# A fused attention and feed-forward kernel on one core: a new hand-stored instruction order, with some copies moved to other engines and one batch's transposes moved to TensorE

## The chip, the cores and the metric

The kernel runs on one core of one Trainium2 chip. The metric is the device time of one launch in microseconds, the median of several runs. A profile of a single execution comes with it; its span runs from the first to the last instruction, and the time of that execution is a little longer than its span.

## What is computed

Linear attention with an exponential feature map, followed by a feed-forward layer with a squared ReLU:

```python
def phi(x):
    proj = np.einsum('bhsd,df->bhsf', x, w_phi)
    proj = proj - np.max(np.abs(proj), axis=-1, keepdims=True)
    return np.concatenate([np.exp(proj), np.exp(-proj)], axis=-1)
q_p, k_p = (phi(q), phi(k))
kv = np.einsum('bhsf,bhsd->bhfd', k_p, v)
z = np.sum(k_p, axis=2)
num = np.einsum('bhsf,bhfd->bhsd', q_p, kv)
den = np.einsum('bhsf,bhf->bhs', q_p, z)[..., None] + 1e-06
x = (num / den)              # to tokens x 512
out = maximum(x @ w_in, 0)**2 @ w_out
```

There are 8 batches of 8 heads, 576 positions and 64 channels per head, 128 features; 4608 tokens, model width 512, hidden width 2048. Inputs and output are float32, and the matmuls take bf16.

## The kernel before

One batch of attention is loaded at a time by GpSimd's DMA queue, which also casts to bf16: `xk`, `xv`, `xq` (L346). For batch 0 the loads are split, k0 into three (the third is half of it). The weights `win` (L364) and `wout` (L369) are loaded in two halves each. A batch's 36 units of 64 positions by two heads are handled in five groups: four of 8 units and one of 4.

Per batch:
- k and q are transposed to `kT` and `qT`. For batches 0 and 1 this is done by TensorE against an identity (L425) with a copy out of PSUM: k by L438 on DVE, or L441 on ACT for the groups below `KTD` of batch 0, and q by L433 on DVE. For later batches SP issues a transposing DMA (L414).
- the features of k: a 64-row matmul with `wphi` (L483), the largest absolute value on DVE (L494), and exponentials on ACT into `kph`. There are two ways. The first `FG` groups of batches 0 and 1 take the exponential straight from PSUM (L527, 512 wide, four per group), and put the scale on v instead: a small exponential (L534) and a multiply on GpSimd (L542) make two scaled `va`. The other groups subtract the maximum on DVE into `ksh` (L504) and take the exponential from there (L512, two per group); their `va` is a plain copy with a column of ones (L465, L466).
- `kv` by 64-row matmuls (L575), in two halves of heads (hf 0 and hf 1), copied by ACT or DVE (L590, L594). A half is issued as four lots of 18 matmuls.
- per pair of position blocks: the features of q (L621, exponentials L628 on ACT; L653 and a maximum on DVE, L660 or L674, then a small exponential), then numerator and denominator (L721), and a scale, a reciprocal and a product on DVE (L731, L738, L742) into `xo`.
- each 128 tokens of `xo` are transposed to `xT`: for batches below `XPE` by TensorE (L752) with a copy by ACT (L757), for the others by a transposing DMA that SP issues (L761).

The feed-forward part runs through nine chunks of 512 tokens: `ffn_in` (L783, then ReLU on ACT L788 and the square on GpSimd L791, or DVE L794 for the last chunks), and `ffn_out` (L814, sixteen 512-column matmuls per 128 tokens in four parts, copied out by DVE L831 and stored by SP L836). For chunk 0 the first `ffn_in` groups cover 128 tokens each, so that they can start as soon as one `xT` is there.

The order of the work is not that in which the code states it. The code makes a list of numbered operations, each with an engine, and `ORDER` is a table of all their numbers. `play` goes through this table and issues each operation; so the table fixes each engine's own order, and with it which ring buffer each operation gets. A negative number −n in the table stands for n warm-up matmuls (L379) that compute nothing. The table holds 56 of them, 55 ahead of the first `ffn_in` group. Costs, due times and pacing edges in the code (such as `pl.after`) were used in making the table; they don't add instructions. The waits between engines follow from which buffers the operations read and write.

In the old table, ahead of the first `xT` copy (L757), ACT has 1 kT copy, 12 L527, 6 L534, 2 full and 2 half L512, 16 L628, 2 L590 and 2 L668.

Of the kernel before, what the change touches and what calls it, by code (L numbers as in the profile page):

```python
# [44 lines left out]
class Plan:  # L45
# [48 lines left out]
    7 9 11 13 15 6 1 2 8 10 17 4 5 -17 35 -2 37 36 38 19 12 52 53 56 -1 63 54 65 55 68 -2 43 39 41 40 -2 74 64  # L94
    69 59 70 42 18 76 75 66 77 58 81 67 80 83 57 -2 85 86 87 44 72 78 79 88 89 -14 45 90 46 92 20 -1 49 50 47
    48 -4 107 112 111 91 93 128 131 114 113 -2 133 134 135 61 94 132 129 110 130 109 108 14 16 21 71 51 23 73
    25 82 60 -4 97 95 84 62 103 96 98 102 175 27 29 31 100 115 136 22 33 104 99 101 106 149 176 177 105 150 151
    24 385 26 137 116 138 -1 142 121 139 170 117 118 122 143 123 119 140 141 120 124 125 144 145 152 171 172
    153 174 173 -3 196 197 146 126 127 154 155 198 156 191 147 148 1442 178 199 1443 193 194 192 -1 210 211
    1435 28 1448 214 215 236 237 225 157 195 1449 179 180 238 226 227 239 240 1445 1446 245 243 184 185 1451  # L100
    387 1444 1450 389 1452 231 230 181 212 1436 158 213 186 163 1437 241 232 229 246 1447 244 1454 182 183 159
    164 160 165 187 188 161 166 162 167 30 32 247 248 249 1439 242 1455 228 234 1438 1456 1440 200 168 169 263
    264 189 250 190 265 1441 1457 254 256 252 253 251 1458 258 201 259 205 1464 1460 1463 1465 266 267 1453 235
    233 255 1461 257 206 260 262 261 216 202 218 207 220 217 219 208 268 270 269 271 221 327 388 222 209 203
    204 280 1467 273 272 1462 224 1459 1466 223 328 284 282 283 329 281 275 285 286 287 274 277 301 330 304 288
    276 279 278 306 302 307 308 309 303 305 34 1471 289 1475 294 1482 290 295 1476 1483 322 310 315 323 325 324
    326 311 296 291 316 297 292 298 293 1478 317 312 318 319 313 314 386 299 320 321 300 390 391 393 401 407
    405 403 1490 336 348 350 349 337 1479 1491 1480 343 345 3 347 346 344 1492 1486 1481 331 338 339 364 366
    369 1485 371 370 367 368 351 372 365 1489 357 1472 1493 1494 1468 352 1473 1474 1503 1469 1470 1504 1505
    1484 358 359 1514 332 340 353 333 354 334 355 360 356 361 378 379 335 1487 1500 1499 373 374 1501 1515 1502  # L110
    413 1516 1488 394 392 419 414 416 409 404 402 410 406 408 411 415 1496 380 1506 1510 375 420 376 381 377
    421 1513 1517 412 559 1511 1497 417 1518 418 1520 1521 382 395 396 1507 478 479 424 425 480 473 426 1498
    1512 561 1523 1529 1536 422 423 475 1508 476 477 563 1509 1524 474 427 428 397 341 362 398 429 431 430 363
    1543 342 1537 1544 1538 1477 399 1522 383 400 434 435 500 1550 502 1551 501 1525 481 482 1539 1545 1546
    1519 433 432 1553 1554 436 562 1540 1541 438 437 442 456 439 458 457 441 451 445 440 443 452 454 444 448
    446 447 495 449 453 450 1526 1577 483 488 484 489 560 1555 587 503 499 1527 459 498 460 455 496 497 504
    1542 1528 1552 1495 384 1581 485 1585 490 486 491 487 492 1547 505 510 461 506 511 462 1533 466 507 512 513
    467 1534 463 464 508 1530 468 1548 1531 1549 1535 1532 1589 564 567 565 577 581 575 493 509 514 515 469 465
    470 471 579 568 1590 544 517 520 522 518 521 524 546 523 545 519 566 1559 1563 593 594 595 588 539 494 472
    516 583 576 578 582 580 584 585 525 526 543 541 547 1595 1599 548 1567 542 540 549 554 532 527 1603 589 596  # L120
    597 1607 533 555 534 528 529 556 1571 590 1574 591 1575 535 1608 550 557 536 1572 530 592 1564 1565 551 552
    553 558 531 1582 1583 1576 586 735 1578 630 632 625 628 626 569 570 598 599 1566 1584 737 1586 631 1579 629
    627 1604 1587 1605 600 1606 1580 739 1588 602 571 573 1609 1573 1591 537 572 1568 574 652 653 608 603 604
    605 738 1560 1561 601 1613 1617 1569 1570 654 606 1600 1601 655 1602 633 1556 1557 1592 607 610 609 612 611
    614 674 616 613 676 675 677 1562 1558 620 615 618 617 622 619 1593 621 624 634 678 647 669 671 670 656 673
    623 672 736 740 743 741 538 1621 635 1625 636 637 1618 638 1626 639 684 640 679 641 1610 642 685 1596 757
    651 648 649 650 643 680 644 645 1619 657 658 681 682 662 686 663 687 1614 688 683 659 664 660 665 1631 763
    1597 1594 1620 1615 1611 1612 1598 666 661 696 698 691 718 697 692 695 694 1622 1649 1623 693 699 1624 689
    667 742 744 1653 720 719 721 764 766 765 713 769 714 715 716 717 700 722 770 771 768 767 773 1616 1635 1639
    1657 646 668 690 701 706 1661 1643 1644 1662 723 728 724 1646 1632 702 729 1650 1633 1634 725 1636 703 730  # L130
    707 726 708 1651 1647 1652 1648 1637 758 751 759 755 753 754 752 756 760 761 762 909 704 1654 1655 709 731
    732 705 710 727 772 1664 1665 828 830 829 801 802 803 805 804 1656 911 1638 745 746 774 775 776 1694 1628
    1667 1640 1629 1695 831 1696 777 1641 778 913 749 747 748 779 780 781 832 782 1642 1666 1630 750 806 784
    785 1671 1675 1672 1679 1673 912 786 788 1658 1659 1668 867 808 807 1645 711 733 1627 1680 1681 1663 1674
    809 850 852 851 783 787 1669 792 791 789 790 793 794 871 796 795 823 826 798 797 800 799 810 1676 1685 825
    827 824 869 1677 868 870 910 914 915 917 712 811 816 1689 817 812 1690 818 833 834 838 813 814 839 1682 835
    1660 1670 853 1683 1684 937 819 820 840 841 1691 931 1686 1693 836 815 821 842 837 872 845 894 896 873 895
    1697 1698 874 847 854 846 1687 1688 849 848 1721 1703 916 918 889 890 891 943 938 893 892 843 734 822 844
    1678 875 897 1692 898 939 945 944 946 1725 860 855 1707 1711 899 1715 856 1716 1726 1727 1708 1709 1710
    1728 1722 857 1748 861 940 900 1723 947 862 858 859 904 905 863 864 1700 876 877 901 902 878 1724 1736 906  # L140
    882 1701 1749 932 919 925 926 933 927 929 934 928 930 935 1702 1750 936 1085 879 883 1730 941 1731 1737
    1732 884 1718 1699 921 1717 923 885 880 886 903 881 907 908 1740 1719 1741 1087 1720 1738 1742 920 1002 948
    975 949 1003 950 1729 1704 1712 942 978 979 1705 977 1713 1714 976 1004 1089 1733 1734 887 1735 865 922 924
    958 953 955 954 997 1754 1739 952 1001 998 1000 951 1755 957 999 956 1743 1747 1751 959 960 1005 962 1086
    1088 970 963 980 964 1752 981 1756 1024 1025 1026 982 983 966 965 969 972 1019 961 1022 1006 971 974 1090
    1093 1091 1103 866 1757 1744 968 967 984 1007 973 1012 1008 1013 1023 1021 1745 985 1761 990 1765 986 1009
    1014 987 1010 1015 991 988 1011 1016 989 1113 1706 1027 1758 1762 992 993 994 1020 1759 1028 1763 1760 1746
    1766 1046 1041 1068 1048 1047 1070 1769 1770 1069 1044 1767 1071 1768 1045 1043 888 1017 1092 1094 1793
    1775 1119 1063 1042 1066 1065 1072 1067 1064 1120 1114 1115 1116 1779 1783 1797 1764 995 996 1018 1787 1830
    1078 1079 1073 1074 1788 1831 1118 1832 1049 1838 1820 1821 1822 1772 1773 1104 1105 1109 1110 1780 1029  # L150
    1781 1121 1784 1097 1753 1101 1106 1099 1095 1107 1771 1102 1108 1111 1782 1774 1117 1839 1030 1031 1075
    1076 1080 1081 1077 1082 1032 1826 1808 1809 1785 1786 1810 1033 1034 1035 1834 1036 1037 1038 1122 1840
    1123 1112 1259 1261 1098 1096 1124 1129 1130 1131 1801 1812 1813 1050 1827 1835 1828 1805 1811 1794 1815
    1100 1125 1126 1133 1132 1806 1795 1814 1790 1791 1796 1178 1134 1151 1180 1179 1135 1136 1819 1154 1056
# [31 lines left out]
def kernel(  # L186
# [10 lines left out]
    nc = tc.nc  # L197
# [49 lines left out]
    r_ot = ring("ot", 3, [P, DM], F32)  # L247

    KVJ = 1
    FG, VON = (3, 3), ((1, 1), (1, 1))  # L250
    KTD = 1
    N0 = 43, 51
    PAIRS, XPE = 1, 1
# [148 lines left out]
    def attention(b, key):  # L402
# [5 lines left out]
        def transposes(xb, ld, xt, at):  # L408
# [11 lines left out]
            for u0, n in ((0, 16), (16, 16), (32, 4)) if b or at else GRP:  # L420
                w, = banks(1)
# [6 lines left out]
                kk = key(1 + u0 + 4 * at)  # L428
# [43 lines left out]
        for g, (u0, n) in enumerate(GRP):  # L472
            kk = key(2 + 8 * g)
# [452 lines left out]
```

## Time and profile before

| | us |
|---|---|
| median of 3 runs (353.75 to 353.82) | 353.75 |
| the profiled execution | 353.51 |
| its span | 351.74 |
| TensorE busy, of the span | 340.9 |
| VectorE (DVE) busy | 245.3 |
| ScalarE (ACT) busy | 240.8 |
| GpSimd (POOL) busy | 185.9 |
| first L783 matmul starts | 29.04 |

Times in the profile count from the span's start. A row of the table of waits reads: engine and instruction, what ended its wait, total of the wait in us, number of times, longest. A row of the timeline reads: start, length, engine, line, operation, output and inputs, number of instructions merged, and in brackets the idle time of the engine just before it and what ended it. PEld is the load of a matmul's stationary operand. Matmul lengths include their latency, so that those of a stream overlap; the rate is read from one start to the next.

### The profile page before, as it was taken

The numbers are of one execution on the slowest core, as the hardware profiler recorded it, in microseconds if no ns is written. First come the engines' busy times: TensorE is split into PE (matmuls) and PEld (weight loads), VectorE is DVE, ScalarE is ACT, GpSimd is POOL, SyncE is SP. The second block draws the span as 40 slices with busy tenths as digits, with TensorE's granted clock in tenths as the row PEclk, the third lists the DMA queues.
The fourth block names the chain that finished last, engine by engine and source line by source line (L and its number), as shares of the span: only waits on it lengthen the run. The fifth ranks groups of instructions, "written<-read, shape, count | busy, mean of one in ns | idle before, by whom it ended". The sixth has DMA issues, their size and how long they took to land.

```text
span 351.7 us, 10140 instructions
## 1 busy us (share of the span) xinstructions
PE 340.9 (97%) x4040; PEld 198.7 (56%) x4040; DVE 245.3 (70%) x556; ACT 240.8 (68%) x486; POOL 185.9 (53%) x293
## 2 busy tenths in 40 slices
PE   7889999999999999999999999999999999999995
PEld 4568877767655655465455555465445644444453
DVE  3879987698498778884879686956688656612421
ACT  3799999389767987897679757892697736504400
POOL 7494962798445874894596646964565400000000
PEclk9899999999999999999999999999999999999999
DMA  7999993479847947599459874693520632222133
GB/s 105 205 209 208 208 166 62 84 136 181 153 84 131 214 52 94 93 164 168 93 107 199 93 99 83 99 214 89 119 48 2 115 54 31 57 64 62 30 75 75
DMA packets 68975, 39.78 MB, mean 113 GB/s; under 512 B 48704, under 2 KB 63424, under 8 KB 68928
## 3 DMA queue, kind: packets, MB, share of 16 engines
q1 hardware_dynamic: 52896, 20.66, 33.2%
q0 software_dynamic: 15872, 18.35, 33.1%
q8 instruction: 31, 0.51, 0.6%
q10 hardware_dynamic: 160, 0.13, 0.2%
q14 instruction: 16, 0.13, 0.1%
HBM read 36.77 MB, written 9.44 MB: 131 GB/s over the span
## 4 chain that ended last, share of the span: by engine, by line
PE 86%; DMA 4%; DVE 3%; ACT 2%; POOL 2%; issue 1%; SPq 1%; DVEq 0%; ACTq 0%; POOLq 0%
PE one L814 35%; PE one L783 33%; PE one L721 6%; PE one L575 5%; PE one L653 2%; PE one L483 2%; PE one L621 2%; DMA kT<-xk 2%; DMA xk<-in_k_dram 2%; POOL va L542 1%; ACT kph L527 1%; DVE mk L494 1%; PE one L425 1%; ACT qph L628 1%; POOL xk L346 1%
## 5 line engine op out<-in xcount | busy, mean ns | idle before, releaser
L791 POOL TENSOR_TENSOR h<-hr 128x512 bf16<-128x512 bf16 x112 | 114.4, 1039 | 73.4 <-ACT hr L788 69.7
L783 PE MATMUL one<-xT,win 128*128 128x512 bf16 (+2 forms) x768 | 139.6, 326 | 0.2 <-DVE xo L742 0.2
L814 PE MATMUL one<-wout,h 128*128 128x512 bf16 (+1 forms) x592 | 137.8, 373 | 0.8 <-issue 0.8
L788 ACT ACTIVATE hr<-one 128x512 bf16<-128x512 f32 x144 | 83.1, 606 | 62.6 <-PE one L783 50.2
L783 PEld LDWEIGHTS <-win 128*128 128x128 bf16 x768 | 66.2, 98 | 48.3 <-issue 0.8
L628 ACT ACTIVATE qph<-one 128x512 bf16<-128x512 f32 (+1 forms) x160 | 80.2, 580 | 9.8 <-PE one L621 9.1
L814 PEld LDWEIGHTS <-h 128*128 128x128 bf16 x592 | 53.8, 98 | 55.6 <-POOL mq L683 1.1
L512 ACT ACTIVATE kph<-ksh 128x1024 bf16<-128x1024 f32 (+1 forms) x68 | 63.7, 972 | 7.9 <-DVE ksh L504 7.7
L494 DVE TENSOR_REDUCE mk<-one 128x4 f32<-128x512 f32 (+1 forms) x80 | 49.7, 629 | 6.9 <-PE one L483 6.5
L731 DVE TENSOR_TENSOR one<-one,em 128x260 f32<-128x260 f32 (+1 forms) x80 | 32.5, 430 | 23.8 <-PE one L721 20.9
L504 DVE TENSOR_TENSOR ksh<-one,mk 128x512 f32<-128x512 f32 (+1 forms) x68 | 42.8, 629 | 3.1
L721 PEld LDWEIGHTS <-qph 128*128 128x128 bf16 x640 | 31.7, 97 | 18.7 <-issue 1.3
L674 DVE TENSOR_REDUCE m<-one 128x4 f32<-128x512 f32 (+1 forms) x60 | 35.7, 631 | 6.6 <-PE one L653 5.4
L831 DVE COPY ot<-one 128x512 f32<-128x512 f32 x35 | 23.7, 683 | 21.2 <-PE one L814 21.1
L721 PE MATMUL one<-kv_sb,qph 128*128 128x65 bf16 x640 | 35.8, 194 | 0.5 <-DVE kv_sb L594 0.3
L683 POOL COPY mq<-m 64x4 f32<-64x4 f32 x108 | 19.9, 184 | 28.1 <-DVE m L674 24.4
L742 DVE TENSOR_TENSOR xo<-one,rden 128x256 bf16<-128x256 f32 (+1 forms) x80 | 31.6, 417 | 1.3
L575 PE MATMUL one<-va,kph 64*128 64x65 bf16 x1152 | 22.6, 190 | 0.3
L738 DVE RECIPROCAL rden<-one 128x4 f32<-128x4 f32 (+1 forms) x80 | 12.8, 174 | 14.0 <-PE one L721 13.5
L575 PEld LDWEIGHTS <-kph 64*128 64x128 bf16 x1152 | 20.6, 94 | 2.5 <-issue 1.8
L794 DVE TENSOR_TENSOR h<-hr 128x512 bf16<-128x512 bf16 x32 | 12.4, 420 | 13.2 <-ACT hr L788 13.0
L542 POOL TENSOR_TENSOR va<-xv,va 128x512 bf16<-128x512 bf16 x12 | 12.4, 1054 | 6.2 <-ACT va L534 6.2
(47 smaller groups left out, 204.4 us busy)
## 6 DMA issues: line engine op xcount, KB each, us to landing
out_dram<-ot SPq DMA_DIRECT2D x70, 128.0 KB, 2.4
xk<-in_k_dram POOLq DMA_DIRECT2D x7, 576.0 KB, 8.5
xv<-in_v_dram POOLq DMA_DIRECT2D x7, 576.0 KB, 9.9
xq<-in_q_dram POOLq DMA_DIRECT2D x7, 576.0 KB, 13.2
win<-in_moe_w_in_dram POOLq DMA_DIRECT2D x2, 1024.0 KB, 13.5
wout<-in_moe_w_out_dram POOLq DMA_DIRECT2D x2, 1024.0 KB, 17.3
xv<-in_v_dram POOLq DMA_DIRECT2D x2, 288.0 KB, 7.8
xq<-in_q_dram POOLq DMA_DIRECT2D x2, 288.0 KB, 8.7
```

The lines of the kernel that those rows point to most:

```text
L494: nc.vector.tensor_reduce(out=mk.t[:, e, ms], in_=wv(e), axis=AX.X, op=ALU.max, apply_absolute_value=True)
L504: nc.vector.tensor_tensor(out=ksh.t[:, e, : n // 2, :], in0=wv(e), in1=mk.t[:, e, ms].to_broadcast([P, n // 2, Fd]), op=ALU.subtract)
L512: nc.scalar.activation(out=t.t[:, :, : n // 2, :].rearrange("x e i f -> x e (i f)"), in_=ksh.t[:, :, : n // 2, :].rearrange("x e i f -> x ...
L575: nc.tensor.matmul(out=kvp(w, hi)[:, 2 * prl + s], lhsT=kph[g][s].t[r, i % 2, i // 2, :], rhs=va[s if g < nf else 0].t[r, u, : D + 1], sta ...
L628: nc.scalar.activation(out=t.t.rearrange("f (r b) hi p -> f b r hi p", b=2)[:, bk, :, :, lo:hi_], in_=w[bk].t[:, : nj * 256].rearrange("f ...
L674: d1 = [dve(kk, nj * 256, lambda w=w, m0=m0, nj=nj, bk=bk: nc.vector.tensor_reduce(out=m0.t[:, bk, : 2 * nj], in_=w[bk].t[:, : nj * 256].r ...
L721: nc.tensor.matmul(out=w.t[:, z * P : z * P + D + 1], lhsT=qg[s].t[:, h // 2, h % 2, :], rhs=kv[r][0].t[:, z % 2, z // 2, s, :], start=(s ...
L731: nc.vector.tensor_tensor(out=x, in0=x, in1=em.t[lo:hi_, hs].to_broadcast(list(x.shape)), op=ALU.mult)
L783: nc.tensor.matmul(out=w.t[:, y * n : (y + 1) * n], lhsT=win[:, kc, mc * P : (mc + 1) * P], rhs=xT.t[:, a:z, kc, :], start=(kc == 0), stop ...
L788: o = act(key - 4, TCH, lambda: nc.scalar.activation(out=r.t, in_=w.t, func=ACT.Relu), [p_], [w, r])
L791: o = pool(key - 4, 1050, lambda: nc.gpsimd.tensor_tensor(out=t.t, in0=r.t, in1=r.t, op=ALU.mult), [o], [r, t])
L814: nc.tensor.matmul(out=w.t[:, cols], lhsT=h2[c, mc, tt][0].t[:, h2[c, mc, tt][1] :][:, :P], rhs=wout[:, mc, cols], start=(mc == 0), stop=( ...
```

## The change

It replaces the whole table `ORDER`, and five settings:

```diff
-    FG, VON = (3, 3), ((1, 1), (1, 1))
-    KTD = 1
+    FG, VON = (4, 3), ((1, 1), (1, 1))
+    KTD = 3
+    QACT = ()
+    KVD = (0,)
     N0 = 43, 51
-    PAIRS, XPE = 1, 1
+    PAIRS, XPE = 1, 2
...
-                    o = dve(kk, n * 38, lambda w=w, n=n, ms=ms: nc.vector.tensor_copy(
+                    on = (b, u0) in QACT
+                    o = (act if on else dve)(kk, n * 38, lambda w=w, n=n, ms=ms, f=(
+                        nc.scalar.copy if on else nc.vector.tensor_copy): f(
...
-                if b or hi:
+                if b or hi not in KVD:
```

- `FG` 3 to 4 for batch 0: its fourth group of k takes the straight way too (four L527, two L534 and two L542 in place of two L504 and two full L512), and the plain copy L466 covers 4 units in place of 12.
- `KTD` 1 to 3: the kT copies of groups 1 and 2 of batch 0 move from DVE (L438) to ACT (L441).
- `XPE` 1 to 2: the five transposes of `xo` that batch 1 completes move from SP's DMA (L761) to TensorE and ACT (four L752 and one L757 each).
- `QACT` is empty and `KVD` holds 0, so the lines that use them issue what was issued before.

The start of the table before and after:

```diff
-    7 9 11 13 15 6 1 2 8 10 17 4 5 -17 35 -2 37 36 38 19 12 52 53 56 -1 63 54 65 55 68 -2 43 39 41 40 -2 74 64
-    69 59 70 42 18 76 75 66 77 58 81 67 80 83 57 -2 85 86 87 44 72 78 79 88 89 -14 45 90 46 92 20 -1 49 50 47
...
+    7 9 11 13 15 17 6 1 2 4 5 8 -20 35 36 -3 52 10 37 12 38 -1 43 63 19 21 23 54 58 57 53 59 61 39 41 40 65 56
+    -3 74 64 42 72 67 55 66 75 76 44 81 69 80 70 77 -5 85 86 87 94 83 79 91 96 98 97 92 18 -10 45 46 20 49 47
+    14 25 27 29 60 16 22 78 89 68 90 88 100 99 24 73 82 62 51 84 -2 104 102 48 50 118 119 71 103 101 113 139
...
```

In both tables 7, 9, 11 issue the loads of k0, 13 and 15 those of v0, 17 and 19 those of q0, 21 and 23 those of `win`; 25, 27 and 29 issue k1, v1 and the first half of `wout`. 6 makes the identity. 35, 37, 39, 41 and 43 are the transposes of k0's five groups on TensorE (43 is the small last one), and 45, 47 and 49 those of q0. The numbers from 52 on are the features; since the fourth group has more operations now, a number from there on means different operations in the two tables: 52, 63, 74, 85 are the L483 matmuls of the first four groups in both, and the fifth group's is 90 before and 96 after.

What the new table does differently at the start, engine by engine:
- GpSimd issues the first half of q0 ahead of the identity. The second half of q0, both halves of `win`, k1, v1 and the first half of `wout` are issued ahead of the first L542. Before, only the first half of `win` was; its second half, k1 and v1 stood among the L542.
- TensorE does group 0's transposes and features first, then the transposes of group 1 and of the small group (43, which needs the third k0 load), then group 1's features (63). Before, both first groups' transposes and features stood ahead of 43. For L575 the half hf 0 is listed first; before, the lots of both halves were mixed.
- ACT has, ahead of the first `xT` copy, 3 kT copies, 16 L527, 8 L534, 2 half L512, 10 L628, 2 L590 and 2 L668.
- The table holds 50 warm-up matmuls, 49 of them ahead of the first `ffn_in` group. That group is i = 0 of chunk 0 (before: i = 2). One `xo` has been transposed by then (before: two), three L621 and four L653 operations are done (before: five and five), and seven L721 operations (before: eight).

Further on, the table interleaves the attention of batches 1 to 7 with the feed-forward groups in another order. After the first `ffn_in` group it changes 82 times between 64-row matmuls (L483, L575, L621, L653) and the others, as the old one does.

## The prediction

> **What bounds it now.** I read the page first: its engine rows, then the chain that ended last.
>
> ```profile
> PE 340.9 (97%) x4040; PEld 198.7 (56%) x4040; DVE 245.3 (70%) x556; ACT 240.8 (68%) x486; POOL 185.9 (53%) x293
> ...
> PE 86%; DMA 4%; DVE 3%; ACT 2%; POOL 2%; issue 1%; SPq 1%; DVEq 0%; ACTq 0%; POOLq 0%
> ```
>
> TensorE is busy for 97% of the span and holds 86% of the chain, so only TensorE's own work and its few holes count. But "busy" includes the latency of each matmul, so I laid the matmuls' starts in the timeline end to end. Four 512-column matmuls start 0.86 us after the four before them, and the 65-column ones of L721 29 ns apart. Priced so, all matmuls other than the warm-up ones (L379) need 316 us. The last matmul starts at 347.7. The remaining 31.7 us split as follows. Before the first FFN group (29.04 in the timeline) only 9.0 us of useful matmul work has been done: 20.1 us lost, warm-ups included. After that the matmul stream changes 82 times between 64-row and 128-row operands, at about 0.11 us each (L621 to L814 costs 0.12, L783 to L653 0.11): 9.0. The rest, 2.7, is real waiting, and most of it lies in three places: 0.39 at 56.2, 0.50 at 81.4, 0.94 at 90.2.
>
> The table of waits names what the last two waited for, from the weight loads' side, and the table for TensorE's matmuls alone the first:
>
> ```profile
> PEld L814 <- POOL mq L683: 1.1, 1, 1.1
> ...
> PEld L483 <- DMA kT<-xk: 0.6, 1, 0.6
> ```
>
> ```profile
> PE one L783 <- DVE xo L742: 0.2, 1, 0.2
> ```
>
> The windows of 10 us show what lies beside the head (columns: window, sum, then PE, PEld, DVE, ACT, POOL busy, the granted TensorE clock, DMA share, GB/s):
>
> ```profile
> 0.00:10.00 10.00, 6.91 (x54) 4.74 (x55) 2.97 (x9) 4.07 (x7) 6.25 (x14) 0.97 0.79 114
> 10.00:20.00 10.00, 8.54 (x96) 5.50 (x94) 9.67 (x20) 7.86 (x19) 6.73 (x9) 0.86 1.15 210
> 20.00:30.00 10.00, 8.93 (x244) 6.85 (x242) 8.18 (x22) 9.62 (x25) 6.58 (x8) 1.00 1.18 208
> 30.00:40.00 10.00, 9.97 (x195) 9.21 (x193) 9.32 (x23) 9.60 (x27) 8.21 (x9) 1.00 1.23 208
> 40.00:50.00 10.00, 9.91 (x253) 7.91 (x251) 9.28 (x21) 9.42 (x23) 9.72 (x12) 1.00 1.22 208
> ```
>
> From 20 to 50 us ACT is full (9.4 to 9.6 of 10). DMA is at its ceiling (about 208 GB/s) from 10 to 50 us, so loads land in the order in which they are queued, whenever they are issued. The ACT timeline of the head has three idle gaps, then runs without one to the first xT copy:
>
> ```profile
> 7.70 2.28 ACT L527 ACTIVATE kph<-one 128x512 bf16<-128x512 f32 x4 [1.21 <-DVE mk L494]
> ...
> 11.24 0.24 ACT L534 ACTIVATE va<-mk 128x8 bf16<-128x8 f32 x1 [1.14 <-DVE mk L494]
> ...
> 12.93 1.08 ACT L527 ACTIVATE kph<-one 128x512 bf16<-128x512 f32 x2 [1.00 <-DVE mk L494]
> ...
> 24.16 4.34 ACT L628 ACTIVATE qph<-one 128x512 bf16<-128x512 f32 x8
> 28.34 0.65 ACT L757 ACTIVATE xT<-one 128x512 bf16<-128x512 bf16 x1
> ```
>
> **The change, part by part.** Order, FG and KTD act on the head together, so I price the head as one: what ACT has listed ahead of the first xT copy (L757). Before: 43 instructions from 5.89 to 28.34, that is 22.45 us, of which 1.21 + 1.14 + 1.00 = 3.35 idle and 19.1 work. After, read off the new list: two more kT copies (L441, 0.60 each: +1.2); four more L527 (0.55 apart: +2.2) and two more L534 (+0.3) for the fourth group; two full-width L512 less (2.05 for two: −1.9 at their pitch); ten L628 where there were sixteen (4.34/8 = 0.54 each: −3.2). Sum −1.4: 17.7.
> - Start: one q load is now issued on POOL ahead of the identity. It takes 0.73 like the other issues, so the identity, the first transposes, and ACT's first copy come 0.73 later, at 6.62.
> - Idle: ACT now waits from 7.2 to 8.2 for the second kT transposes. PE's list puts the transposes of group 4 (third k load, which PE waits for until 9.30 today) ahead of group 1's features, and L441 for group 2 waits for that load until about 10.5 (0.3). After that DVE, which loses two kT copies (0.42 each) and two subtractions (0.69 each), stays ahead. I take 1.3 idle where 3.35 was.
> - So the first xT copy starts at 6.62 + 17.7 + 1.3 = 25.6 and the first FFN group 0.70 later (29.04 − 28.34), at 26.3.
> - POOL: two more multiplies (L542, 1.05 each), a plain copy a third as long, and the win, k1, v1 and wout issues ahead of all multiplies instead of among them. Issues of 0.73 to 0.9 from 5.9 on are done by 10.7; eight multiplies and a 0.4 copy then end at about 20, against 21.82 now. The hf0 half of L575 is listed first and needs only the first three groups. Not the bound.
>
> At the first FFN group the new list has 8.0 us of useful PE work behind it, the old one 9.0: lost time 18.3 instead of 20.1, −1.8. Six L628 (3.2 us of ACT) are moved behind it. The FFN groups listed there and ACT's fuller use hide most of that; I charge 0.3, and without that cover it costs up to 3.2. **Head: −1.5** (from −2.4 to +2.0).
>
> **x of batch 1 on PE (XPE 2).** Five groups of four transposes: L752's transposes start 55 ns apart in today's four groups, and the next L783 group starts 0.27 us after the first of them. I charge 0.24 a group: **+1.2** on PE, uncovered. Five ACT copies of 0.60 to 0.65: 3.0 on ACT, at 40 to 75 us, hidden by ACT's idle (0.96 in 50 to 60, 5.0 in 60 to 70) unless they fall before 50. Five DMA transposes leave SP (about 1.3 us of issue each). They stand among batch 2's transposes on SP's queue:
>
> ```profile
> 71.94 1.26 SPq L761 DMA_TRANSPOSE xT<-xo  x1
> ...
> 74.52 1.28 SPq L414 DMA_TRANSPOSE kT<-xk  x1
> ...
> 77.19 1.69 SPq L761 DMA_TRANSPOSE xT<-xo  x1
> ```
>
> L483 then waits for kT of batch 2 at 81.4. That 0.50, and the 0.39 at 56.2 where an FFN group waits for an xT, should go: **−0.9**. What comes late next is the ACT copy of xT, whose nearest FFN group stands 0.8 us behind its transposes in the new list.
>
> On this price a rule speaks against the change. The Trainium skill, "TensorE: Matmul & The Clock Gate", Part 4, gives a 128x128 transpose on TensorE about 275 ns inside a kernel. By it the twenty transposes would be estimated at 5.5 us and the sum into a loss of some 3 us; today's L752 rows show 55 ns from start to start, and the measurement decides.
>
> **Steady stage.** The new list has the same 82 row changes after the first FFN group, the same FFN work, and about as few places where a consumer stands close behind its producer. The POOL wait at 90.2 (a 2.10 us copy L466 and 1.78 us of L683 ahead of the h squares) can return anywhere: I leave it as it is, **0**, between −0.9 and +2. KVD and QACT change no instruction. Six fewer warm-ups (50 for 56) stand where PE waits anyway.
>
> Sum: −1.5 + 1.2 − 0.9 = −1.2. The profiled execution takes 353.51 (span 351.74 and 1.77 around it), so 352.3. The median of the three runs is 353.75, 0.24 above it, which gives 352.5.
>
> **Rivals.**
> - Given back (0.25): the head comes 1.5 earlier, but ACT, already 94 to 96% busy up to 50 us, pays for the six moved L628 there and PE waits again. For: those windows. Against: less DVE work, and a list with more FFN ahead of the batch 1 features. 353.75 + 1.2 − 0.9 = 354.05; same.
> - ACT becomes the bound (0.13), slower: ACT gains 1.2 + 2.2 + 0.3 − 1.9 + 3.0 = 4.8 us. Its idle time between 20 and 60 is 0.38 + 0.40 + 0.58 + 0.96 = 2.3. If all of it must be done before 60 us, 2.5 falls on PE: 353.75 + 1.2 + 2.5 = 357.4. It decides when ACT's waits in that stage go to zero.
> - The early k0 plan fails (0.10): the late identity and group 1 behind the third k load cost 0.73, and the three ACT gaps stay. 353.75 + 0.73 + 1.2 − 0.9 = 354.8; slower.
> - Better (0.07): the POOL wait vanishes too and the head gives 2.4: 350.7.
>
> **How the numbers follow.** My forecast has 0.45, the four rivals the chances beside them. Its own range is 351.3 to 353.0: the bounds of the head that still leave a gain. About 0.2%, 0.7 us, is what a measurement of this kernel can tell from no change. Faster: 0.45 + 0.07 = 0.52; same: 0.25; slower: 0.13 + 0.10 = 0.23. The range, 350.7 to 355.2, reaches from the better case past the failed k0 plan and leaves out the ACT rival and the far ends of the others, some 0.17.
>
> **What would show it.** Right: first L783 group near 26.3, kph of the last group by 20 us, no L483 wait for kT near 81, twenty L752 more at 55 ns. Wrong: ACT without idle from 20 to 60 and PE waiting for ACT there; a first FFN group after 28.5; long POOL or SP waits past 100 us.

## The result, and the profile after

The new kernel takes 366.03 us (median of 361.89 to 367.44) against 353.75: ratio 1.0315, 95% interval [1.0225, 1.0406]. It is slower by 3%; the forecast was 352.5, faster by 0.35%. The ratio is taken over the runs in the fast state alone, so it is not the quotient of the two medians. The profiled execution is the quickest one, 361.89 with a span of 360.0. What follows explains that execution; why the other three were 3.5 to 5.6 us longer, no profile shows.

Lines of the new kernel stand 2 lower down in the code than in the old one up to about L433, and 4 lower after it (L783 is L787, L814 is L818, L761 is L765, L483 is L487). The first two lines on the page of the new kernel that answer to those of before are TensorE's row and the chain:

```profile
PE 340.5 (95%) x4019; PEld 199.1 (55%) x4054; DVE 244.2 (68%) x552; ACT 243.5 (68%) x497; POOL 187.6 (52%) x295
...
PE 80%; DMA 7%; DVE 6%; POOL 3%; issue 2%; another core or an unknown queue 0%; SPq 0%; ACT 0%; DVEq 0%; POOLq 0%
```

TensorE has the same busy time as before (340.9) in a span that is 8.2 longer. So it waits. TensorE's share of the chain falls from 86% to 80%. The table of waits of the new kernel for TensorE names two:

```profile
PE one L787 <- issue: 6.1, 1, 6.1
PE one L487 <- DMA kT<-xk: 1.9, 1, 1.9
```

Before, that table's longest wait past 30 us was 0.8 (0.96 between weight loads, as the budget below counts). The head, by contrast, went better than forecast. In the windows of the new kernel (same columns as before) TensorE's clock is whole from 10 to 20 us (0.86 before) and ACT has no idle there. The whole clock is not the new order's doing: of eleven profiles that have this head, four show 3.4 us of half clock between 8.8 and 14.9 us, and in these four the first FFN group comes latest (25.73 to 26.08; in the other seven 24.75 to 25.58).

```profile
10.00:20.00 10.00, 8.09 (x188) 5.87 (x187) 8.73 (x19) 10.00 (x28) 9.58 (x12) 1.00 1.15 209
20.00:30.00 10.00, 9.50 (x206) 7.92 (x203) 9.38 (x26) 9.44 (x24) 3.87 (x5) 1.00 1.18 208
...
40.00:50.00 10.00, 9.89 (x231) 7.46 (x233) 7.54 (x18) 9.71 (x23) 9.90 (x13) 1.00 1.13 187
```

ACT's timeline runs from its first kT copy to the first xT copy, and TensorE's first FFN group follows at 24.96 (29.04 before):

```profile
6.59 0.60 ACT L445 ACTIVATE kT<-one 128x512 bf16<-128x512 bf16 x1 [4.57 <-PE one L427]
...
24.18 0.73 ACT L761 ACTIVATE xT<-one 128x512 bf16<-128x512 bf16 x1
```

```profile
24.96 1.05 PE L787 MATMUL one<-xT,win 128*128 128x128 bf16 x16
```

**The long wait.** Three views of the new kernel, read side by side, show it. TensorE stands still from 136 to 142.65, and the next 12 matmuls take 4.74 us (11 of the same width before the wait 2.75):

```profile
133.78 2.75 PE L818 MATMUL one<-wout,h 128*128 128x512 bf16 x11
142.65 4.74 PE L787 MATMUL one<-xT,win 128*128 128x512 bf16 x12 [6.12 <-issue]
147.23 1.03 PE L818 MATMUL one<-wout,h 128*128 128x512 bf16 x4
```

The group needs an xT that SP issues last of three, at 132.77:

```profile
127.96 1.26 SPq L416 DMA_TRANSPOSE kT<-xk  x1
129.32 4.64 SPq L765 DMA_TRANSPOSE xT<-xo  x3
134.07 1.46 SPq L840 DMA_DIRECT2D out_dram<-ot  x2
```

Around it, from 131.96 to 134.25, GpSimd issues the loads of batch 5, 576 KB of source each:

```profile
131.96 0.80 POOL L348 DMA_DIRECT2D xk<-in_k_dram  x1
132.76 0.75 POOL L348 DMA_DIRECT2D xv<-in_v_dram  x1
133.49 0.76 POOL L348 DMA_DIRECT2D xq<-in_q_dram  x1
```

The tile's view gives the time from issue to landing (shortest, median, longest) of the xT between 130 and 147 us, and of the kT between 94 and 112 us:

```profile
DMA to landing us min/median/max: 3.2/4.0/9.8
```

```profile
DMA to landing us min/median/max: 9.1/10.1/11.2
```

The xT issued at 132.77 landed at 142.56, and TensorE went on at 142.62. The kT issued at 96.25 landed at 107.45, and TensorE went on at 107.50. The page calls the first wait "issue", because it infers releasers and found none; but the group reads the xT of 132.77, and it starts 0.06 after that one landed. The granted clock is in the windows (the last three columns: clock, DMA share, GB/s):

```profile
130.00:136.00 6.00, 5.94 (x52) 2.99 (x51) 5.86 (x13) 3.03 (x5) 4.25 (x5) 1.00 0.70 89
136.00:142.60 6.60, 0.53 (x3) 0.04 (x1) 4.74 (x8) 1.06 (x1) 0.00 (x0) 0.79 1.21 191
142.60:147.00 4.40, 4.35 (x11) 1.56 (x12) 0.00 (x0) 0.68 (x2) 0.00 (x0) 0.53 1.14 233
```

**A budget that closes.** I split the time up to the last matmul's start into four parts: the start of the first FFN group; the gaps after it (TensorE's weight loads more than 0.6 us apart, less 0.2 for the pitch of the widest); half of the time in which the clock was at one half outside those gaps; and the rest. For the old kernel this is 28.95 + 1.5 + 0 + 317.3 = 347.7, for the new one 24.90 + 8.5 + 2.0 + 320.3 = 355.7. So the change brings −4.05 at the head, +3.0 in the rest (work moved behind the head or added, and waits too short to count as gaps), +7.0 of gaps and +2.0 of slow clock. The −4.05 compares unlike heads: the old kernel's profile has 3.4 us of half clock in it, the new one's none. Like with like the head leads by 2.7 to 3.0 (means of the profiles with that half clock, 28.6 and 25.9, and without, 28.1 and 25.1). Every experiment below is read in these four parts.

### The profile page after: what moved, and what is told of

Its sections match the earlier page's. It is cut to its first block, busy times and chain, and to the rows that moved or that the text cites. A ratio compares the mean times of both kernels' runs of the same rounds, so it can differ in the third digit from the quotient of the medians.

```text
span 360.0 us, 10117 instructions
## 1 busy us (share of the span) xinstructions
PE 340.5 (95%) x4019; PEld 199.1 (55%) x4054; DVE 244.2 (68%) x552; ACT 243.5 (68%) x497; POOL 187.6 (52%) x295
## 3 DMA queue, kind: packets, MB, share of 16 engines
q1 hardware_dynamic: 50176, 20.00, 29.5%
## 4 chain that ended last, share of the span: by engine, by line
PE 80%; DMA 7%; DVE 6%; POOL 3%; issue 2%; another core or an unknown queue 0%; SPq 0%; ACT 0%; DVEq 0%; POOLq 0%
PE one L787 34%; PE one L818 28%; PE one L725 5%; PE one L579 5%; DMA kT<-xk 3%; PE one L657 2%; PE one L625 2%; POOL va L546 2%; PE one L487 2%; DMA xv<-in_v_dram 2%; DMA out_dram<-ot 1%; DVE one L735 1%; DVE xo L746 1%; DVE mk L498 1%; DVE ksh L508 1%
## 5 line engine op out<-in xcount | busy, mean ns | idle before, releaser
L787 PE MATMUL one<-xT,win 128*128 128x512 bf16 (+2 forms) x768 | 141.1, 329 | 6.3 <-issue 6.1
L818 PE MATMUL one<-wout,h 128*128 128x512 bf16 (+1 forms) x557 | 134.3, 373 | 2.1 <-issue 0.3
L787 PEld LDWEIGHTS <-win 128*128 128x128 bf16 x768 | 65.9, 98 | 54.7 <-issue 10.4
L818 PEld LDWEIGHTS <-h 128*128 128x128 bf16 x592 | 54.2, 98 | 56.3 <-issue 1.9
L516 ACT ACTIVATE kph<-ksh 128x1024 bf16<-128x1024 f32 (+1 forms) x66 | 62.3, 967 | 6.3 <-DVE ksh L508 6.2
L498 DVE TENSOR_REDUCE mk<-one 128x4 f32<-128x512 f32 (+1 forms) x80 | 49.7, 630 | 19.0 <-PE one L487 16.8
L678 DVE TENSOR_REDUCE m<-one 128x4 f32<-128x512 f32 (+1 forms) x60 | 36.2, 631 | 12.1 <-PE one L657 10.5
L508 DVE TENSOR_TENSOR ksh<-one,mk 128x512 f32<-128x512 f32 (+1 forms) x66 | 41.4, 627 | 3.3
L835 DVE COPY ot<-one 128x512 f32<-128x512 f32 x35 | 23.8, 683 | 11.2 <-PE one L818 8.8
L579 PE MATMUL one<-va,kph 64*128 64x65 bf16 x1152 | 21.8, 190 | 0.4 <-POOL va L546 0.2
L742 DVE RECIPROCAL rden<-one 128x4 f32<-128x4 f32 (+1 forms) x80 | 12.7, 173 | 11.5 <-PE one L725 10.9
L487 PE MATMUL one<-wphi,kT 64*128 64x128 bf16 x288 | 14.5, 218 | 2.9 <-DMA kT<-xk 1.9
```

The costliest lines, as they stand in the source:

```text
L498: nc.vector.tensor_reduce(out=mk.t[:, e, ms], in_=wv(e), axis=AX.X, op=ALU.max, apply_absolute_value=True)
L508: nc.vector.tensor_tensor(out=ksh.t[:, e, : n // 2, :], in0=wv(e), in1=mk.t[:, e, ms].to_broadcast([P, n // 2, Fd]), op=ALU.subtract)
L516: nc.scalar.activation(out=t.t[:, :, : n // 2, :].rearrange("x e i f -> x e (i f)"), in_=ksh.t[:, :, : n // 2, :].rearrange("x e i f -> x ...
L579: nc.tensor.matmul(out=kvp(w, hi)[:, 2 * prl + s], lhsT=kph[g][s].t[r, i % 2, i // 2, :], rhs=va[s if g < nf else 0].t[r, u, : D + 1], sta ...
L678: d1 = [dve(kk, nj * 256, lambda w=w, m0=m0, nj=nj, bk=bk: nc.vector.tensor_reduce(out=m0.t[:, bk, : 2 * nj], in_=w[bk].t[:, : nj * 256].r ...
L787: nc.tensor.matmul(out=w.t[:, y * n : (y + 1) * n], lhsT=win[:, kc, mc * P : (mc + 1) * P], rhs=xT.t[:, a:z, kc, :], start=(kc == 0), stop ...
```

## The experiments

Theory 1: transposing DMAs that SP issues beside a batch's loads land late, and the new order gives them too little room. The main rival: the new order is worse in itself. A second mechanism came up on the way, as theory 2: TensorE's own program is fetched by DMA too, and late beside loads. In the expectations of b5late, b45late, splice1 and before_x2, written before it came up, "theory 2" is another one, that ACT has too much to do, and "theory 3" is many small waits.

| kernel | median us | ratio to the old one, 95% | first FFN | gaps | half clock | rest |
|---|---|---|---|---|---|---|
| old | 353.75 | | 28.95 | 1.5 | 0 | 317.3 |
| new | 366.03 | 1.0315 [1.0225, 1.0406] | 24.90 | 8.5 | 2.0 | 320.3 |
| b5late | 365.64 | 1.0289 [1.0223, 1.0355] | 25.26 | 10.9 | 4.5 | 321.7 |
| b45late | 363.45 | 1.0251 [1.0207, 1.0294] | 25.57 | 8.1 | 2.4 | 321.8 |
| splice1 | 363.72 | 1.0272 [1.0221, 1.0322] | 24.75 | 11.4 | 5.6 | 318.1 |
| before_x2 | 363.54 | 1.0286 [1.0235, 1.0338] | 28.31 | 7.9 | 0 | 320.1 |
| after_x1 | 391.39 | 1.1086 [1.1021, 1.1152] | 24.99 | 35.5 | 9.7 | 318.6 |
| before_shift | 368.76 | 1.0425 [1.0373, 1.0478] | 30.45 | 10.1 | 5.0 | 318.0 |
| before_thin | 351.79 | 0.9936 [0.9905, 0.9967] | 28.27 | 0 | 0 | 317.6 |
| after_thin | 354.91 | 1.0061 [1.0031, 1.0092] | 25.45 | 4.7 | 0 | 320.2 |
| after_spread | 364.72 | | 26.08 | 8.5 | 2.2 | 321.1 |
| before_spread | 357.81 | 1.0124 [1.0074, 1.0174] | 27.95 | 6.0 | 0 | 317.5 |
| before_shift_spread | 364.71 | 1.0303 [1.0254, 1.0353] | 31.20 | 6.7 | 2.8 | 318.1 |
| before_x2_spread | 360.89 | 1.0214 [1.0177, 1.0252] | 28.51 | 7.4 | 1.4 | 320.2 |
| before_noload | 351.44 | 0.9951 [0.9933, 0.9970] | 27.80 | 0 | 0 | 317.4 |
| after_noload | 352.92 | 0.9998 [0.9971, 1.0026] | 25.82 | 0 | 0 | 320.6 |
| shift_noload | 355.58 | 1.0061 [1.0038, 1.0084] | 30.24 | 0.5 | 0 | 318.5 |
| after_place | 363.71 | 1.0280 [1.0229, 1.0331] | 25.73 | 9.1 | 3.2 | 320.6 |
| after_pext | 355.98 | 1.0058 [1.0016, 1.0099] | 25.00 | 3.5 | 0 | 322.2 |
| after_fix | 355.73 | 1.0056 [1.0022, 1.0089] | 25.93 | 1.5 | 0 | 322.1 |

The last four columns are in us, from each kernel's profiled execution; b5late's is its longest run, 368.29. after_spread's four runs lay between 356.5 and 370.9, too far apart for a ratio.

**b5late and b45late: move the loads that meet the late transposes.**

```diff
-... 768 915 917 919 1690 ... 1698 837 ...
+... 768 1690 ... 1698 915 917 919 837 ...
```

> The changed kernel, with only the three load issues of batch 5 moved on GpSimd's list behind the squares of the three feed-forward groups that wait for the xT transposes. Theory 1 (late landings: a transposing DMA that is issued while loads are in flight lands after 10 us instead of 2.5, and the new order leaves no margin for it): the 6.1 us wait near 136 and the half clock behind it go, the xT lands in 2.5 to 4 us, 353 to 356 us. Theory 2 (the settings: ACT has too much to do): no change, 361 to 367. Theory 3 (many small waits all over the new order): at most 1 us off.

b45late also puts 745, 741 and 743 (loads of batch 4, q first) behind 593, the plain va copy of batch 3.

> As the run before, and the loads of batch 4 moved too, behind the plain v copy of batch 3 and with q first, so that they are not in flight when the last two kT transposes of batch 3 are issued. Theory 1: both the wait near 136 and the 2 us wait for kT near 105 go; 351 to 354 us. Theories 2 and 3: as for the run before.

The named waits went, 136 in the first, 105 in the second, but the time did not: a kT of batch 5, whose load now comes later, is waited for at 162.4 and 156.5 us (5.3 each), and b5late waits 4.05 at 99 for an xT. Where a load moves, another transfer of the new order is caught. That fits theory 1 but doesn't yet rule out its rival.

**splice1 and before_x2: one part of the change alone.** splice1 has the first 342 entries of the new table and the remaining operations in the old order; before_x2 is the old kernel with one setting changed.

```diff
-    PAIRS, XPE = 1, 1
+    PAIRS, XPE = 1, 2
```

> The first 342 entries of the new table (up to the first feed-forward groups and a little beyond), then everything that is left in the order of the old table; FG 4 and KTD 3 as in the change, but XPE 1 as before. Theory 1: the new head keeps its gain of about 3 us (first feed-forward group near 25 us) and the old tail has the old margins; 350 to 351.5 us. Theory 2: ACT's work that the new head puts off makes TensorE wait between 30 and 60 us; 353 to 356.

> The old kernel and table with XPE 2 alone: the five transposes of batch 1's xo go from SP to TensorE and ACT, in the same places of the table. By the prediction's terms plus 1.2 for the transposes and minus 0.9 for the two waits: 354.0 us, that is 353.2 to 355. Theory 2: ACT cannot take the five copies before 75 us; 356 or more.

Each part alone costs about 10 us, which no expectation of splice1 had, and more than before_x2's. Two waits of splice1 are of the known kind (3.98 for an xT, 1.75 for a kT), but its 3.65 at 200 us, and 1.47 at 165 us and 2.59 at 241 us in before_x2, stand at matmuls whose inputs had all been there for 2 us and more when TensorE went on. So theory 1 is not all. The other long wait of before_x2, 1.99 at 82 us, is the one that its expectation's theory 2 names: the FFN group goes on 0.05 after ACT's copy of its xT has ended, 3.9 us behind TensorE's transposes. And TensorE now waits for xo itself (0.9 at 55 us), where SP waited before:

```profile
PE one L783 <- ACT xT L757: 1.8, 1, 1.8
...
PE one L752 <- DVE xo L742: 1.0, 2, 0.8
```

**after_x1: the new order with batch 1's transposes back on SP.**

```diff
-    PAIRS, XPE = 1, 2
+    PAIRS, XPE = 1, 1
```

> The new kernel with batch 1's twenty transposes back on SP's transposing DMA (XPE 1, same order). By the forecast's own step this takes 1.2 us off TensorE. Theory 1: the two waits at 105 and 136 us stay, since they belong to later batches: 359 to 365, within 3 us of the new kernel either way. Rival (the transposes on TensorE are the cause): 353.

Neither: 391.4, with six waits of 1.2 to 10.5 us between 59 and 172 us, all for xT or kT, and one of 1.1 at 233 us of the kind that the next run shows. The new order was made with those five transfers off SP's queue; put back, they delay what stands behind them on it (read from the order of the queue, not tested by itself). In the new order the step that the forecast priced at +1.2 is worth about −25 us.

**before_shift: the old order, only its program shifted.** 36 narrow warm-up matmuls (16 columns) in place of the first 17, and 14 more in a wait at 7.5 us:

```diff
-... 4 5 -17 35 -2 37 ... 65 55 68 -2 43 39 ...
+... 4 5 -1036 35 -2 37 ... 65 55 68 -2 -1014 43 39 ...
```

> The old kernel and old order, with only the rows of TensorE's program shifted: the first 17 warm-up matmuls (256 columns) become 36 narrow ones (16 columns), and 14 more narrow ones stand in the 1.5 us wait at 7.5 us. Everything after stands 66 rows later in TensorE's program, about a quarter of the 256 rows that one instruction fetch brings; transfers and waits keep their order. Theory 2 (TensorE's fetches are late when they fall into a burst of loads, and the old order has them fall well): new gaps of 1 to 4 us at matmuls that wait for no semaphore, with a fetch inside them; 355 to 362. Theory 1 alone (only transposes are late): 353 to 354.5.

This was the surprise: 15 us slower, more than even theory 2 allowed, with nothing changed past 10 us but the place of each instruction in TensorE's program (and what follows from it: the head, too, comes 1.5 later). The waits view and a piece of TensorE's timeline:

```profile
PE one L577 <- issue: 9.2, 3, 3.8
```

```profile
243.97 0.35 PE L577 MATMUL one<-va,kph 64*128 64x65 bf16 x12
248.08 0.27 PE L577 MATMUL one<-va,kph 64*128 64x65 bf16 x6 [3.75 <-issue]
```

L577 (L575 of the old kernel) stops in the middle of a lot of 18 with all its operands there. The page's list of DMA queues has a row for it:

```profile
q8 instruction: 32, 0.52, 0.6%
```

32 packets of 16 KB. TensorE's program has 4073 matmuls here, each with its weight load, so 8146 rows, some 255 to a packet (31 packets for the new kernel's 8108). In the trace, packets of this queue end at 51.06, 90.84, 165.71 and 246.63 us; TensorE's four gaps after 30 us end at 52.52, 92.28, 167.19 and 248.07, that is 1.44 to 1.47 us after each packet. They stand behind rows 1726, 2748, 4536 and 6326: 4, 7 and 7 times 256 apart, but for 2 to 4 rows. The same holds for before_x2 (1.34 and 1.51 at 165 and 241 us), splice1 (1.26 at 200 us) and after_place (1.47 at 88 us); all these gaps stand 182 to 190 rows past a multiple of 256. TensorE had run out of instructions.

The old kernel has one such stall too, the 0.96 at 90.2 us that the prediction put down to POOL. It stands behind the same row 2748, in the middle of a group of four, whose squares on POOL had ended by 79.1; TensorE goes on at 91.36, 1.31 after a packet's end. The copy that the table of waits names was over at 90.40:

```profile
88.62 1.78 POOL L683 COPY mq<-m 64x4 f32<-64x4 f32 x8
```

**Loads cut, then left out.** Both kernels and the shifted one. The thin kernels load a quarter of k, v and q of batches 2 to 7, the others nothing of them; they compute on what older batches left in the buffers.

```diff
+        e = a + 1 if b >= 2 else z
...
-                in_=rows[:, a:z, :],
+                in_=rows[:, a:e, :],
```

> The old kernel, with each load of batches 2 to 7 cut to a quarter of its bytes (one of the four head pairs; the rest of the tile keeps the values of an older batch, so this kernel leaves out part of the input). Order, waits and instructions stay. Theory 1 (the new kernel loses its time to small transfers, the transposing DMAs and TensorE's own instruction fetches, that land late while a batch's loads are in flight): the old kernel has only 1.5 us of TensorE gaps after 30 us, so 351.5 to 353.5. Rival (loads in flight cost nothing, the new order is worse in itself): 353.5.

> The new kernel with the same cut of the loads of batches 2 to 7 to a quarter. Theory 1: the 2.0 us wait at 105 us and the 6.5 us wait at 136 us (with its 1.7 us of half clock behind) are gone, and no gap over 0.5 us stands in their place after 30 us; 351 to 353, so at or under the thinned old kernel, since the head is 3.1 us better and the extra transposes on TensorE cost 1.3. Rival (the order itself, or what any change of it does): 360 to 366, as with the full loads.

```diff
         def fn():
+            if b >= 2:
+                return
```

> The old kernel with no loads at all for batches 2 to 7 (it computes on what batches 0 and 1 left in the buffers, so the input of those batches is left out). Order, transposes, stores and all engines' work stay. Theory (transposing DMAs and instruction fetches are late only beside loads): gaps after 30 us stay under 1 us, 350 to 351.5, that is 2 to 3 us under the old kernel.

> The new kernel with no loads for batches 2 to 7 (same part of the input left out). Theory: the waits at 99, 105 and 136 us are under 1 us each and no half clock follows, so what is left is the forecast's own sum, first group 4 us earlier, 1 us of useful work given up for it and 1.2 us for the extra transposes: 348 to 350.5, 1 to 2 us below the old kernel without loads. Rival (the order has too little room for the transposes even when they land in 2.4 us): 354 or more, as with the quarter loads.

> The shifted old kernel (368.8 us with loads) with no loads for batches 2 to 7. Theory 2 (the fetch is late because loads are in flight): the gaps of 2.1, 3.3 and 3.8 us and their half clock go; 351.5 to 354, as its head is about 1.5 us later than the old kernel's and pays one half clock there. Rival (a fetch at such a row stalls by itself): 362 or more.

With a quarter of each load the new order still waits 1.4 and 3.3 us for two xT; with none it has no wait over 0.4 us after 30 us. The first lines of its waits are all in the head:

```profile
PE one L429 <- DMA xk<-in_k_dram: 1.8, 1, 1.8
PE one L383 <- DVE ones L317: 1.2, 1, 1.2
PE one L429 <- POOL ident masks.py:199: 0.8, 1, 0.8
PE one L489 <- ACT kT L447: 0.4, 1, 0.4
```

shift_noload loses the gaps too (10.1 to 0.5): without loads one fetch is 0.5 late, and no other shows. So the loads in flight cost the new order its 8.5 + 2.0 us; in its own profile both gaps are waits for transposes, none is a fetch. The rival that the order has too little room even for a free DMA falls. What was wrong in the expectation: the new order is not faster than the old one even here (352.92 against 351.44). Its head lead is only 2.0 us here, because now its own profile has the half clock in the head and the old one's has none, and its rest is 3.2 longer.

**Loads halved and spread.** Those of batches 3 to 7 in two halves each, 4 to 10 us apart where their buffers allowed it.

```diff
+            if n[-1] == "+":
+                o = Op()
+                o.eng, o.fn = "pool", self.more[int(n[:-1])]
+                yield o
...
-        def fn():
+        def fn(a=a, z=a + 2 if b in SPLIT else z):
```

> The new kernel with the loads of batches 3 to 7 cut into halves (288 KB of the source each instead of 576), issued one by one some 4 to 10 us apart and up to 40 us earlier, as soon as the older batch has left its buffer, in place of three loads within 2 to 8 us. TensorE's, ACT's and DVE's order and the bytes moved stay; 15 more DMA issues on POOL, 0.75 us each, off the path. Theory (bursts of loads make the transposing DMAs and TensorE's instruction fetches 7 to 11 us late): the waits at 105 and 136 us and the half clock behind them go, transposing DMAs land in under 5 us after 70 us; 349.5 to 352, below both kernels. Rival (the total traffic is what counts, or the order itself): 358 to 366.

> The old kernel with the loads of batches 3 to 7 halved and spread in the same way. It has 1.5 us of TensorE gaps after 30 us to give: theory 352 to 353.5 (same as before within 0.3 per cent). Rival (any change of this order of work finds some fetch or transpose that is late): 358 or more.

> The old kernel with its program shifted by 66 rows (368.8 us, gaps of 2.1, 3.3 and 3.8 us at the edge of a late instruction fetch and 5.1 us of half clock behind them) and the loads spread. Theory: the fetches come in time again wherever they fall, and the three gaps and the half clock behind them go; 353.5 to 356 (its head is 1.5 us later and stays so). Rival (the shift itself costs the time, whatever the loads do): 365 to 370.

> The old kernel with batch 1's transposes on TensorE (363.5 us, gaps of 7.9 us after 30 us) and the loads of batches 3 to 7 spread. Theory: gaps under 2 us, the extra transposes cost 1.2 to 1.5 us: 353.5 to 356. Rival: 360 to 364.

The theory missed in all four; after_spread and before_x2_spread fell where the rival had them. The fetch stalls did shrink where the halves were far apart (before_shift: 3.34 to 0.91 at 164 us, 3.77 to 0.47 at 244), not where batch 3's six halves still came within 10 us (2.09 to 3.83 at 90). But a half load still delays a transpose: after_spread's xT of 134.3 landed 8.0 us later, and TensorE waited 4.9. The old kernel lost 4 us by it, most of it in one wait of 3.4 at 93 us for an exponential of ACT (its L640). The chain behind that is in the trace: ACT waited 4.61 for POOL's copies (L695), and these stood behind the plain va copy (L478), which had waited 4.35 for the late half of v.

**after_place: whole loads, in places picked from the trace.**

```diff
-... 741 ... 743 ... 745 ... 915 917 919 ...
+... 741 742 ... 745 746 ... 743 744 ... 919 920 ... 915 916 917 918 ...
```

> The new kernel with whole loads, only those of batches 4 and 5 issued elsewhere: k and q of batch 4 at 81 us instead of 96 to 103, its v at 107, q of batch 5 at 111 and its k and v at 139 instead of 132 to 133, so that no load is in flight when the xT of 95 us, the kT of 96 us or the xT of 133 us is issued (4 to 11 us before its first use). Theory 1: the waits at 105 and 136 us go; 351 to 354.5, if no instruction fetch is caught in the new bursts. Theory 2 (any burst may catch a fetch): one or two gaps of 1 to 4 us without a semaphore, at other places; 354 to 359. Rival (the order itself): 361 to 366.

The kT wait at 105 went. But a fetch was caught at 88 beside the moved loads (2.90 without a semaphore). SP's xT moved from 132.8 to 136.8, and the loads of batch 5 came at 136.2 and 137.0: they met again, it landed 9.2 us later, and TensorE waited 5.66. Theory 2's stall came, but not its time: 363.71 lies above its 359, in the range of the rival, and the larger part of it is theory 1's kind of wait.

**after_pext and after_fix: the loads stay, the transposes leave.**

```diff
-            if hi_ == P and b < XPE:
+            if hi_ == P and (b < XPE or (c, tt) in ((3, 1), (3, 3))):
```

with the two pairs of operations (651, 652 and 695, 696) placed among the L818 matmuls just before the group that reads them.

> The new kernel with only two of its transposes changed: the two xT of chunk 3 that SP issues at 131.4 and 132.8 us, 9.9 us and less ahead of the wait at 136 us, are made by TensorE (8 transposes, 0.4 us) and copied by ACT. All loads stay where they are. Theory 1 (a transposing DMA beside three loads takes 10 us and the new order gives this one 3.3 us): the 6.5 us wait and the 2.0 us of half clock behind it go, the 2.0 us wait for kT at 105 us stays; 353.5 to 357, against 361.9 to 367.4 for the new kernel. Rival (the wait only moves on to the next late transfer or fetch): 359 to 365, with another gap of over 3 us within the next 30 us.

> The same, and the loads of batch 4 issued behind the va copy of batch 3, some 3 us later and q first, so that the two kT of 96 and 98 us are issued before them. Theory 1: the wait at 105 us goes too; gaps under 2 us after 30 us, 352 to 355, near the old kernel: the head's 4.05 us less 3.0 us of work moved behind it or added. Rival (theory 2, any burst catches some fetch): a gap of 1 to 4 us without a semaphore, 355 to 360.

This is the test of theory 1 at its main place: two xT, eight TensorE transposes, nothing else, and the new kernel falls from 366.03 to 355.98 (the profiled executions from 361.89 to 356.44). In after_pext TensorE's timeline runs through the place (the 6.12 before the FFN group is now 0.68 ahead of the transposes):

```profile
136.71 0.38 PE L758 MATMUL one<-ident,xo 128*128 128x128 bf16 x4 [0.68 <-DVE ksh L510]
137.15 1.67 PE L820 MATMUL one<-wout,h 128*128 128x512 bf16 x7
138.66 2.75 PE L789 MATMUL one<-xT,win 128*128 128x512 bf16 x12
```

The kT wait of 1.9 is still in after_pext and gone in after_fix, as expected. Both end 0.6% slower than the old kernel, in the middle of what was expected for the first and above it for the second: their rest is 1.8 us longer than the new kernel's, of which the eight transposes explain 0.4. Small waits of 0.4 to 0.8 are part of it, and the waits table of after_fix names what they are for, operations that ended 0.05 us before and free the PSUM bank that TensorE writes next:

```profile
PE one L489 <- ACT hr L794: 0.7, 1, 0.7
PE one L758 <- DVE ksh L510: 0.7, 1, 0.7
```

No version that computes the whole result beats the old kernel.

## Why the prediction was wrong

- **The bound** (TensorE and its holes) was right, and the whole result is holes.
- **Head, −1.5**: right in its mechanism. ACT's first copy came at 6.59 (6.62 forecast), but the first xT copy at 24.18, not 25.6: 0.8 idle and 16.8 of work where 1.3 and 17.7 were reckoned. Lost time before the first group is 17.0, not 18.3. The full clock from 10 to 20 us was not in the sum, and it is luck of this execution: like with like the first group comes 2.7 to 3.0 earlier, where the sum had 2.7 (29.04 to 26.3). The "ceiling" of DMA at about 208 GB/s is none: the window from 142.6 to 147 above has 233.
- **XPE 2, +1.2**: about right for the transposes. In after_noload 24 more of them (L752) stand behind the first FFN group and take 1.3 us by the matmuls' starts and 1.8 by the weight loads', so twenty take 1.1 to 1.5. What had no price is that TensorE then waits itself for xo and for ACT's copies (0.9 and 2.0 in before_x2, none of that length in the new kernel). The Trainium skill's figure ("TensorE: Matmul & The Clock Gate", Part 4) would have given 5.5, which no run shows.
- **Two later waits, −0.9**: they went, and the wait at 90.2 with them, but two of the three were misread. The group at 56.2 had its xT by 41.1 and went on 0.05 after DVE's product (L742) ended, which reads the PSUM bank that the group writes; the one at 90.2 was a late fetch. So 0.39 of this term came true by luck, and what the sum called a POOL wait that "can return anywhere" was a sign of the fetches.
- **KVD, QACT, ACT as the bound**: nothing came of them; ACT has 0.3 to 0.75 idle in each window from 20 to 60.
- **Steady stage, 0: the step that failed.** I wrote that the new list has "about as few places where a consumer stands close behind its producer", and bounded this by −0.9 and +2. I had followed consumers of DVE, ACT and POOL only, and left out SP's transposing DMAs, whose landing time isn't fixed. In the traces, the room from issue to first use (including any wait) of those issued between 30 and 260 us is under 6 us for 1 of 85 in the old order (5.9) and for 10 of 79 in the new (down to 3.0). The view that would have warned was in front of me: before's own xT and kT took up to 10.9 and 8.0 us to land. That the old kernel paid next to nothing for them was a matter of room: the kT issued at 74.5 landed 7.4 later and was taken 7.5 after issue (TensorE waited 0.3 for it), and the xT that took 10.9 had 29.5.
- The prediction's last line named "long POOL or SP waits past 100 us" as what would show it wrong. That is what came, but with no chance and no price in the sum: 7.0 of gaps and 2.0 of half clock, where the bound said +2.
- What is left without these waits stays between two readings. The profiled run's budget gives −4.05 + 3.0 − 1.5 (the old order's own gaps) = −2.5, but with heads compared like with like (−2.7 to −3.0) it is −1.2 to −1.5, about the −1.2 of the sum. No kernel shows it: those that did lose the waits are behind the old one, after_noload by 1.5 us against before_noload (some 0.8 of it goes with the half clock in its head, and the old order's 1.5 of gaps is gone there too), after_fix by 0.6%. Their rest is 3.2 and 4.8 longer than that of the old order, where the sum had 2.5 (transposes 1.2, work moved behind the head 1.0, ACT 0.3).

Open: why the new kernel's runs differ by 5 us, and what queue or limit makes a fetch start late.

## What to carry to other kernels

Before you price a new order, list each DMA that a tight engine waits for, with the time from its issue to its first use, and hold it against the longest landing that the trace of today shows, not the median. An order that looks equal by engine work can be 3% apart by which small transfers it puts beside large loads. And test how fragile a kernel is before believing a gain or a loss of 3%: shift its program by a few dozen harmless instructions and see what the time does.

## What the runs showed of the hardware

- **Landing beside loads.** In both traces, past 53 us, a transposing DMA lands in 2.5 us (median of 71 and 72; up to 5.3) with no load in flight in its first 2.4 us, in 2.4 to 6.6 with one, 2.4 to 11.2 with two and 4.0 to 11.5 with three. A load's packets take 0.107 us each, a transpose's 0.018 (medians). The Trainium skill, "DMA: Bandwidth & Descriptors", "Queues, rings and completion order", says that each DMA engine goes round between its queues a packet at a time; transposes that slow down without stopping agree with this.
- **TensorE's instructions come by DMA**, 16 KB for about 256 rows, and TensorE restarts 1.3 to 1.5 us after a late packet has ended. The seven stalls of 2 us and more in these runs stood where loads had just been in flight, most of them among or just behind short matmuls (L575, L721), where 256 rows pass quickest (72 L575 with their loads in 1.31 us in splice1; 12 L783 in 2.75). Moving the program by 66 rows cost 15 us.
- **The clock.** From 4 us into the 6.5 us wait the clock was at one half for 6.8 us, 4.1 of them beside work. Waits of 2.0 (before_x2_spread), 2.1 (before_shift) and 2.9 (after_place) were followed by 3.4 us of half clock, others of 2.0, 2.6 and 3.3 by none. The Trainium skill, "TensorE: Matmul & The Clock Gate", "Why this matters for your kernels", gives about 3 us of idle time as what the clock bears; here 2.0 was enough once.
